# Attention with a top-32 mask: y from the sign tile, reciprocal behind it, scores four steps ahead, turns behind the product with v

## The chip, the cores and the metric

One core of a Trainium2 chip runs the kernel. The metric is device time in microseconds; before the change the median of 3 runs is 1154.14 us (1153.25 to 1154.17). The profile is of one further execution, with a span of 1156.5 us.

## The reference

Attention over 8 batches and 8 heads, 576 positions, head size 64. For each query only the scores not below the 32nd largest count. The result, as 4608 tokens of 512 features, goes into a mixture of 8 experts with a capacity of 80 tokens each.

```
scores = scale * q @ k.T
kth    = 32nd largest of each row of scores
attn   = softmax(where(scores >= kth, scores, -1e9))
x      = (attn @ v), heads side by side            # 4608 x 512
expert = argmax(x @ w_gate); of each expert the 80 tokens of largest gate weight are kept
out    = gate_w * (relu(x @ w1[e]) @ w2[e])        # 0 for the others
```

## The kernel before, in words

**Tiling.** Two heads are taken together: 32 head pairs n. A pair has four full row tiles t = 0 to 3 (128 query rows of two heads) and a tail tile t = 4 (64 rows of each head in one tile of 128). A full tile is two *units*, one a head (h = 0 and 1); the tail is one unit (h = 2). So a pair is nine units and there are 288. A unit is a matrix of 128 rows by 576 scores in f32.

**What is done with a unit.**

- `turn` (L169, L170, L180): TensorE turns q and k of a pair (natural layout) and ScalarE copies them out as qT and kT.
- `front` (L192, L197): TensorE forms the scores of a tile (two units) in a PSUM tile of four banks, of which there is one (`ps_s`, by `four()`); ScalarE copies them, scaled by 2^-48, into an SBUF tile `s`. The turns and the gate logits use the same PSUM tile.
- `parts` (L204): VectorE takes the top 8 of each of six chunks of 96, which makes 48 candidates, in six instructions (the letters G of the step).
- `search` (L215, L223): three rounds of max and match_replace on the candidates give the 24th value w9[7]. Behind the last round ScalarE forms `sign` = Sign(w9[7] - s) with its sum `cnt` (L220), which tells how many scores lie below. VectorE then forms y (L226), s where s < w9[7] and 0 elsewhere; takes y's top 8 (L228); and picks by `cnt` which of the nine values is the 32nd (`pick`, L231). That goes into `thr_all`.
- `below` (L239): GpSimd (POOL) compares s with the threshold: `mask`.
- `turn_w` (L271, L276, L278, L280): TensorE transposes s into PSUM (`ab`, one buffer, and `cc`, two), subtracts the mask by a product with `minus`, and ScalarE takes exp of it: wT.
- `back` (L294): the product of wT with v and a column of ones, into `cc`; the last column holds the sums of the softmax.
- `over` (L306): VectorE takes the reciprocals of the sums, z. `divide` (L315): ScalarE scales the product by them, xn.
- `norm` (L321 to L341): xn is stored, turned, and multiplied by the gate's weights (logits, L332), in pieces spread over steps.

**The order.** It is written out by hand (`tc.manual_schedule`): each engine executes its instructions in the order in which the program issues them. `run` goes through steps i; each brings one unit into the search and carries earlier units onward. The string of letters in `step` is the order on VectorE: G is one of the six chunk maxima of unit i; a to e are the rounds of the search; y, g and h are y, its max and the pick; m is the mask on POOL, and z the reciprocals. `back` tells for each letter how many units behind i its unit is. After the letters come TensorE's and ScalarE's parts of the step. Before the change: turn_w (unit i-3), divide, then, in steps without scores, the turn of the next pair or a piece of norm, then front (unit i+3) and back (unit i-4).

With nine units in a pair and these distances, some steps hold a turn and the product together, and there the turn stands ahead of the product in TensorE's queue.

**Stages.** Attention runs to about 986 us. The routing follows (selection of 80 tokens an expert, to about 1050 us), then the experts. At the end a branch on `bad` would run a slower version (`lean`), which is not executed with these data.

Of the kernel before, what the change touches and what calls it, by code (L numbers as in the profile page):

```python
# [9 lines left out]
F32 = mybir.dt.float32  # L10
BF16 = mybir.dt.bfloat16
# [3 lines left out]
Alu = mybir.AluOpType  # L15
# [10 lines left out]
def kernel(  # L26
# [11 lines left out]
    nc = tc.nc  # L38
    B, H, S, D = q.shape
# [8 lines left out]
    P = 128  # L48
    HP = H // 2
    NP = B * HP  # L50
    NF = S // P
# [8 lines left out]
    NU = NP * UPP  # L60
# [58 lines left out]
    class Attention:  # L119
# [62 lines left out]
        def front(self, n, t):  # L182

            qT, kT = self.turned[n]
            m = P if t < NF else TL
            i = n * UPP + 2 * t
            ps = self.four()
            for j in range(2):
                for h in range(2):
                    d = slice(D * h, D * h + D)  # L190
                    o = ps[:, 2 * h + j, :HS] if t < NF else ps[TL * h : TL * h + TL, j, :HS]
                    nc.tensor.matmul(o, lhsT=qT[d, t * P : t * P + m], rhs=kT[d, j * HS : (j + 1) * HS], start=True, stop=True)  # L192
            g = 2 if t < NF else 1
            s = self.rows.tile([P, 2 * S], F32, name="s", tag="s", bufs=2 if self.lean else 4)
            for h in range(g):
                self.s[i + h] = s[:, h * S : (h + 1) * S]
            nc.scalar.activation(s[:, : g * S].rearrange("p (j c) -> p j c", c=HS), ps[:, : 2 * g, :HS], Act.Copy, scale=TINY)  # L197
# [10 lines left out]
        def search(self, i):  # L208

            s, cand = self.s[i], self.top[i]  # L210
            top = self.top[i] = self.small.tile([P, G0 // 8 - 1, 8], F32, name="top", tag="top")
            w9 = self.small.tile([P, 16], F32, name="w9", tag="w9")
            for r in range(G0 // 8):
                dst = top[:, r, :] if r < G0 // 8 - 1 else w9[:, :8]
                nc.vector.max(out=dst, in_=cand)  # L215
                if r == G0 // 8 - 1:

                    sign = self.rows.tile([P, S], BF16, name="sign", tag="sign", bufs=1)
                    cnt = self.small.tile([P, 1], F32, name="cnt", tag="cnt")
                    nc.scalar.activation(sign, s, Act.Sign, bias=w9[:, 7:8], scale=-1.0, accum_out=cnt)  # L220
                yield
                if r < G0 // 8 - 1:
                    nc.vector.match_replace(out=cand, in_to_replace=dst, in_values=cand, imm_value=LOW)  # L223
                    yield
            y = self.rows.tile([P, S], F32, name="y", tag="y")
            nc.vector.scalar_tensor_tensor(out=y, in0=s, scalar=w9[:, 7:8], in1=s, op0=Alu.is_lt, op1=Alu.mult)  # L226
            yield
            nc.vector.max(out=w9[:, 8:], in_=y)  # L228
            yield
            pick = self.small.tile([P, TOP_K - G0 + 1], F32, name="pick", tag="pick")  # L230
            nc.vector.scalar_tensor_tensor(out=pick, in0=past, scalar=cnt, in1=w9[:, 7:], accum_out=self.thr[:, i : i + 1],  # L231
                                           op0=Alu.is_equal, op1=Alu.mult)
            yield
# [7 lines left out]
        def search_all(self, i):  # L241

            s = self.s[i]
            top = self.top[i] = self.small.tile([P, TOP_K // 8, 8], F32, name="top", tag="top")
            scr = self.rows.tile([P, S], F32, name="y", tag="y")
            nc.vector.max(out=top[:, 0, :], in_=s)
            for r in range(1, TOP_K // 8):
                nc.vector.match_replace(out=scr, in_to_replace=top[:, r - 1, :], in_values=s if r == 1 else scr,
                                        imm_value=LOW)
                nc.vector.max(out=top[:, r, :], in_=scr)  # L250
            nc.vector.tensor_copy(self.thr[:, i : i + 1], top[:, TOP_K // 8 - 1, 7:8])
# [126 lines left out]
        def run(self, slow):  # L378

            units = []  # L380
            for n in range(NP):
                for t in range(NF):
                    units += [(n, t, 0), (n, t, 1)]
                units.append((n, NF, 2))
            first, second = {}, {}
            later = []
            due = []
            drawn = []
            ready = {}

            def whole(i):

                return 0 <= i < NU and units[i][2] > 0

            def step(i, last):
                if 0 <= i < NU:
                    n, t, h = units[i]
                    if t == 0 and h == 1 and 0 < n and n + 1 < NP:
                        self.load(n + 1, *divmod(n + 1, HP))
                    if t in (1, 3) and h == 0 and slow and n:  # L400
                        slow.pop(0)()
                    if t == 1 and h == 0 and n + 1 < NP:
                        due.append(n + 1)
                    first[i] = self.parts(i)

                back = dict(a=0, b=1, c=1, d=1, e=1, y=1, g=2, h=3, m=3)
                for c in "GhmbGcGdGeGGgazy":
                    if c == "G":
                        if 0 <= i < NU:
                            next(first[i])  # L410
                    elif c == "a":
                        if 0 <= i < NU:
                            next(first[i], None)
                            second[i] = self.search(i)
                            next(second[i])
                    elif c == "z":
                        for u in drawn:
                            self.over(*u)
                    elif c == "m":
                        if 0 <= i - back[c] < NU:  # L420
                            self.below(i - back[c])
                    elif i - back[c] in second:
                        next(second[i - back[c]])
                busy = False
                if whole(i - 3):
                    self.turn_w(*units[i - 3][:2])
                ends = []
                for u in drawn:
                    self.divide(*u)
                    if u[1] == NF:  # L430
                        ends.append(u[0])
                drawn.clear()
                fronts = 0 <= i + 3 < NU and units[i + 3][2] != 1
                if not fronts:
                    if due:
                        self.turn(due.pop())
                        busy = True
                for g in list(later):
                    if ready[g] and (fronts or busy) and not last:
                        continue  # L440
                    busy = busy or ready[g] == 1
                    ready[g] = next(g, None)
                    if ready[g] is None:
                        later.remove(g)
                for n in ends:
                    b, hp = divmod(n, HP)
                    later.append(self.norm(n, b, hp, b % 2, 2))
                    ready[later[-1]] = 0
                if fronts:
                    self.front(*units[i + 3][:2])  # L450
                if whole(i - 4):
                    self.back(*units[i - 4][:2])
                    drawn.append(units[i - 4][:2])

            with tc.manual_schedule():
                self.load(0, 0, 0)
                self.load(1, *divmod(1, HP))
                nc.sync.dma_start(wg, moe_w_gate.rearrange("(c p) e -> p c e", p=P))
                self.turn(0)
                i = -3  # L460
                while i < NU + 5 or later:
                    step(i, i > NU + 5)
                    i += 1
            assert not slow and not due

# [277 lines left out]
```

## Time and profile before

| engine | busy us | share of the span | instructions |
|---|---|---|---|
| PE (TensorE) | 921.9 | 80% | 13262 |
| DVE (VectorE) | 999.5 | 86% | 5218 |
| ACT (ScalarE) | 714.0 | 62% | 1534 |
| POOL (GpSimd) | 520.7 | 45% | 344 |

The shares are means over stages of different kinds, so that the stretches by time matter more than this table. Median distance from one y to the next in attention is 3.25 us, the length of a step. The costliest groups on VectorE are these; a line has engine, operation, output and inputs with their shapes and the count, then busy us and mean ns of one, then the idle time just ahead of the group and what ended it.

```profile
L204 DVE MAX8 cand<-s 128x8 f32<-128x96 f32 x1728 | 395.2, 242 | 8.8 <-ACT s L197 8.8
L215 DVE MAX8 top<-cand 128x8 f32<-128x48 f32 x576 | 108.0, 187 | 0.1
L223 DVE MATCH_REPLACE8 cand<-top,cand 128x48 f32<-128x48 f32 x576 | 107.8, 187 | 0.0
L306 DVE RECIPROCAL z_all<-cc 128x2 f32<-128x2 f32 x128 | 19.8, 155 | 32.8 <-PE cc L294 32.6
```

The last figure of L306 is time in which VectorE stood idle in front of the reciprocals, nearly all of it until the product L294 had ended. (The same instruction on the 64-row tails is a form of its own.)

### The profile page before, as it was taken

Reading aid. Unit: us, or ns where it says so; the run is one execution under the profiler, and the core shown is the slowest. Engines: PE = TensorE matmul, PEld = TensorE weight load, DVE = VectorE, ACT = ScalarE, POOL = GpSimd, SP = SyncE. Lnnn points to the kernel's source line nnn. Section 1 sums busy time; section 2 is a strip of 40 time slices with the busy share of each in tenths; the row PEclk is TensorE's granted clock in tenths of the full one; section 3 lists DMA queues with packets and bytes.
Section 4 is the critical chain, followed back from the end, with each engine's and each line's share of the span. In section 5 each row is a group of like instructions: output and inputs, shape, how many; then the busy total and the mean of one; then the engine's idle time right before and its main releaser. Section 6 shows DMA issues by size and latency. Waiting matters only on the chain.

```text
span 1156.5 us, 35811 instructions
## 1 busy us (share of the span) xinstructions
PE 921.9 (80%) x13262; PEld 753.3 (65%) x13262; DVE 999.5 (86%) x5218; ACT 714.0 (62%) x1534; POOL 520.7 (45%) x344
## 2 busy tenths in 40 slices
PE   6988888888888888888888888888888887207897
PEld 3766766666666666676667676666666666207886
DVE  6999999999999999999899999998999998691011
ACT  4777776777677777767677777776777766100110
POOL 2555554555555545555455545545555455001101
PEclk9999998999999899988999989998999988656999
DMA  4144442323232332332132211111111100402830
GB/s 107 34 115 116 115 116 70 79 79 79 79 79 79 79 79 79 79 79 79 48 81 71 62 33 43 39 42 34 42 43 43 43 12 12 156 0 71 312 128 27
DMA packets 167895, 85.77 MB, mean 74 GB/s; under 512 B 117792, under 2 KB 154656, under 8 KB 167712
## 3 DMA queue, kind: packets, MB, share of 16 engines
q1 hardware_dynamic: 166688, 80.78, 25.4%
q0 software_dynamic: 1024, 2.62, 0.7%
q8 instruction: 106, 1.74, 0.6%
q14 instruction: 77, 0.63, 0.2%
HBM read 63.19 MB, written 20.19 MB: 72 GB/s over the span
## 4 chain that ended last, share of the span: by engine, by line
DVE 49%; PE 26%; issue 12%; ACT 9%; POOL 3%; DMA 0%; SPq 0%; DVEq 0%; POOLq 0%; ACTq 0%
DVE cand L204 17%; PE cc L294 7%; DVE y L226 7%; DVE w L228 6%; DVE cand L223 6%; ACT s L197 4%; DVE top L215 3%; PE yp L651 3%; PE sp L169 3%; ACT wT L280 3%; PE ab L271 3%; POOL mask L239 2%; DVE pick L231 2%; DVE w L215 2%; DVE top L526 1%
## 5 line engine op out<-in xcount | busy, mean ns | idle before, releaser
L239 POOL TENSOR_SCALAR mask<-s,thr_all 128x576 bf16<-128x576 f32 x288 | 496.3, 1723 | 477.7 <-DVE cand L223 453.7
L204 DVE MAX8 cand<-s 128x8 f32<-128x96 f32 x1728 | 395.2, 242 | 8.8 <-ACT s L197 8.8
L220 ACT ACTIVATE sign<-s,w 128x576 bf16<-128x576 f32 x288 | 226.2, 786 | 118.1 <-DVE w L215 114.1
L294 PEld LDWEIGHTS cc<-vb,wT 128*64 128x64 f32 x5760 | 217.5, 149 | 36.9 <-ACT wT L280 20.1
L294 PE MATMUL cc<-vb,wT 128*64 128x65 f32 x5760 | 239.4, 236 | 2.6 <-ACT wT L280 1.1
L226 DVE SCALAR_TENSOR_TENSOR y<-s,w 128x576 f32<-128x576 f32 x288 | 228.8, 794 | 0.2 <-issue 0.2
L228 DVE MAX8 w<-y 128x8 f32<-128x576 f32 x288 | 212.3, 737 | 0.0
L192 PE MATMUL sp<-kT,qT 64*128 64x288 f32 (+1 forms) x1280 | 203.6, 438 | 5.0 <-ACT kT L180 2.5
L271 PE MATMUL ab<-ident,s 128*128 128x128 f32 x1152 | 187.6, 294 | 1.2 <-ACT wT L280 1.2
L197 ACT ACTIVATE s<-sp 128x1152 f32<-128x1152 f32 (+1 forms) x160 | 166.8, 1042 | 16.4 <-PE sp L192 16.2
L271 PEld LDWEIGHTS ab<-ident,s 128*128 128x128 f32 x1152 | 136.5, 149 | 25.8 <-ACT wT L280 14.8
L280 ACT ACTIVATE wT<-ab 128x1024 f32<-128x1024 f32 (+1 forms) x160 | 150.6, 941 | 0.0
L276 PEld LDWEIGHTS <-mask 128*128 128x128 bf16 x1440 | 94.9, 99 | 70.4 <-POOL mask L239 68.1
L192 PEld LDWEIGHTS sp<-kT,qT 64*128 64x128 f32 (+1 forms) x1280 | 106.3, 180 | 43.2 <-ACT s L197 4.1
L278 ACT ACTIVATE wT<-cc 128x256 f32<-128x256 f32 (+1 forms) x160 | 58.8, 368 | 108.8 <-PE cc L276 108.8
L276 PE MATMUL cc<-minus,mask 128*128 128x128 bf16 x288 | 64.4, 223 | 59.2 <-POOL mask L239 59.1
L215 DVE MAX8 top<-cand 128x8 f32<-128x48 f32 x576 | 108.0, 187 | 0.1
L223 DVE MATCH_REPLACE8 cand<-top,cand 128x48 f32<-128x48 f32 x576 | 107.8, 187 | 0.0
L276 PE MATMUL ab<-minus,mask 128*128 128x128 bf16 x1152 | 103.2, 221 | 0.0
L315 ACT ACTIVATE xn<-cc,z_all 128x64 f32<-128x64 f32 (+1 forms) x320 | 82.9, 317 | 1.9 <-DVE z_all L306 1.8
L271 PE MATMUL cc<-ident,s 128*128 128x128 f32 x288 | 81.8, 284 | 0.0
L169 PE MATMUL sp<-ident,xn 128*128 128x128 f32 x128 | 26.4, 341 | 42.5 <-ACT s L197 42.5
(164 smaller groups left out, 861.4 us busy)
## 6 DMA issues: line engine op xcount, KB each, us to landing
w<-in_moe_w_dram SPq DMA_DIRECT2D x32, 512.0 KB, 4.0
w<-in_moe_w_dram SPq DMA_DIRECT2D x8, 2048.0 KB, 13.0
out_dram<-zero SPq DMA_DIRECT2D x9, 1024.0 KB, 5.8
qn<-in_q_dram SPq DMA_DIRECT2D x64, 128.0 KB, 3.8
kn<-in_k_dram SPq DMA_DIRECT2D x64, 128.0 KB, 2.9
vb<-in_v_dram SPq DMA_DIRECT2D x64, 128.0 KB, 2.6
xd<-xn SPq DMA_DIRECT2D x32, 256.0 KB, 2.3
qn<-in_q_dram SPq DMA_DIRECT2D x32, 32.0 KB, 3.4
```

Of the source, the lines that this page charges most:

```text
L192: nc.tensor.matmul(o, lhsT=qT[d, t * P : t * P + m], rhs=kT[d, j * HS : (j + 1) * HS], start=True, stop=True)
L197: nc.scalar.activation(s[:, : g * S].rearrange("p (j c) -> p j c", c=HS), ps[:, : 2 * g, :HS], Act.Copy, scale=TINY)
L204: nc.vector.max(out=cand[:, j, :], in_=s[:, j * S // NG : (j + 1) * S // NG])
L220: nc.scalar.activation(sign, s, Act.Sign, bias=w9[:, 7:8], scale=-1.0, accum_out=cnt)
L223: nc.vector.match_replace(out=cand, in_to_replace=dst, in_values=cand, imm_value=LOW)
L226: nc.vector.scalar_tensor_tensor(out=y, in0=s, scalar=w9[:, 7:8], in1=s, op0=Alu.is_lt, op1=Alu.mult)
L228: nc.vector.max(out=w9[:, 8:], in_=y)
L239: nc.gpsimd.tensor_scalar(self.mask[i], self.s[i], self.thr[:, i : i + 1], None, op0=Alu.is_lt)
L271: nc.tensor.matmul(dst[h][c], lhsT=sc[:, keys[c]], rhs=ident, start=c == 0 or (c == NF and h == 0), stop=False, is_transpose=True, skip_gr ...
L276: nc.tensor.matmul(dst[h][c], lhsT=mk[:, keys[c]], rhs=minus, start=False, stop=True, skip_group_check=True)
L280: nc.scalar.activation(wT[:, : g * NF, :], ab.rearrange("p h c r -> p (h c) r")[:, : g * NF, :], Act.Exp, scale=scale / TINY)
L294: nc.tensor.matmul(cc[r : r + TL, o], lhsT=wT[:, j * NF + c if c < NF else 2 * NF + j, r0 : r0 + TL], rhs=vb[:, c, h, :], start=(c == 0), ...
```

## The change

- y becomes s times sign, a plain product of two tensors: s where it is below the 24th value, 0 at it, -s above, so that the maximum over y is the same as long as the values in question are positive. It no longer needs w9 as a scalar, but needs ScalarE's sign tile. `sign` gets two buffers, y one.
- y, its max, the pick and the mask go one step later (`back` 1, 2, 3, 3 becomes 2, 3, 4, 4), so that a step lies between the issue of the sign and its use. What follows (turn_w, back) goes one step later too.
- The reciprocals (z) stand behind y instead of in front of it.
- The scores are formed four steps ahead instead of three, with five `s` tiles instead of four.
- In a step TensorE's order is turn_w, scores, product, and only then a turn or a piece of norm.
- The loads of q, k and v are issued for pair n+2 in the middle of pair n, where they were issued for n+1 near its start; the turn of the next pair is due two steps earlier.

```diff
-            s = self.rows.tile([P, 2 * S], F32, name="s", tag="s", bufs=2 if self.lean else 4)
+            s = self.rows.tile([P, 2 * S], F32, name="s", tag="s", bufs=2 if self.lean else 5)
...
-                    sign = self.rows.tile([P, S], BF16, name="sign", tag="sign", bufs=1)
+                    sign = self.rows.tile([P, S], BF16, name="sign", tag="sign")
...
-            y = self.rows.tile([P, S], F32, name="y", tag="y")
-            nc.vector.scalar_tensor_tensor(out=y, in0=s, scalar=w9[:, 7:8], in1=s, op0=Alu.is_lt, op1=Alu.mult)
+            y = self.rows.tile([P, S], F32, name="y", tag="y", bufs=1)
+            nc.vector.tensor_tensor(out=y, in0=s, in1=sign, op=Alu.mult)
...
-                    if t == 0 and h == 1 and 0 < n and n + 1 < NP:
-                        self.load(n + 1, *divmod(n + 1, HP))
+                    if t == 2 and h == 1 and n + 2 < NP:
+                        self.load(n + 2, *divmod(n + 2, HP))
...
-                    if t == 1 and h == 0 and n + 1 < NP:
+                    if t == 0 and h == 0 and n + 1 < NP:
                         due.append(n + 1)
...
-                back = dict(a=0, b=1, c=1, d=1, e=1, y=1, g=2, h=3, m=3)
-                for c in "GhmbGcGdGeGGgazy":
+                back = dict(a=0, b=1, c=1, d=1, e=1, y=2, g=3, h=4, m=4)
+                for c in "GhmbGcGdGeGGgayz":
...
-                busy = False
-                if whole(i - 3):
-                    self.turn_w(*units[i - 3][:2])
+                if whole(i - 4):
+                    self.turn_w(*units[i - 4][:2])
...
-                fronts = 0 <= i + 3 < NU and units[i + 3][2] != 1
-                if not fronts:
-                    if due:
-                        self.turn(due.pop())
-                        busy = True
+                busy = 0 <= i + 4 < NU and units[i + 4][2] != 1
+                if busy:
+                    self.front(*units[i + 4][:2])
+                if whole(i - 5):
+                    self.back(*units[i - 5][:2])
+                    drawn.append(units[i - 5][:2])
+                if due and not busy:
+                    self.turn(due.pop())
+                    busy = True
...
-                if fronts:
-                    self.front(*units[i + 3][:2])
-                if whole(i - 4):
-                    self.back(*units[i - 4][:2])
-                    drawn.append(units[i - 4][:2])
```

More of the change, by code (lines that the diff above doesn't have):

```diff
@@ L244, in search_all @@
             top = self.top[i] = self.small.tile([P, TOP_K // 8, 8], F32, name="top", tag="top")
-            scr = self.rows.tile([P, S], F32, name="y", tag="y")
+            scr = self.rows.tile([P, S], F32, name="y", tag="y", bufs=1)
             nc.vector.max(out=top[:, 0, :], in_=s)
@@ L423, in step @@
                         next(second[i - back[c]])
-                busy = False
-                if whole(i - 3):
-                    self.turn_w(*units[i - 3][:2])
-                ends = []
+                if whole(i - 4):
+                    self.turn_w(*units[i - 4][:2])
                 for u in drawn:
                     self.divide(*u)
-                    if u[1] == NF:
-                        ends.append(u[0])
+                ends = [n for n, t in drawn if t == NF]
                 drawn.clear()
-                fronts = 0 <= i + 3 < NU and units[i + 3][2] != 1
-                if not fronts:
-                    if due:
-                        self.turn(due.pop())
-                        busy = True
+                busy = 0 <= i + 4 < NU and units[i + 4][2] != 1
[7 more added lines that the diff above has]
+                    busy = True
                 for g in list(later):
-                    if ready[g] and (fronts or busy) and not last:
+                    if ready[g] and busy and not last:
                         continue
@@ L459, in run @@
                 self.turn(0)
-                i = -3
-                while i < NU + 5 or later:
-                    step(i, i > NU + 5)
+                i = -4
+                while i < NU + 6 or later:
+                    step(i, i >= NU + 6)
                     i += 1
```

## The prediction

> **What bounds the kernel now.** I read the 40 slices and the table of stretches first, then who waited for whom, then the groups of VectorE (DVE), then the timeline around one wait.
>
> ```profile
> PE   6988888888888888888888888888888887207897
> DVE  6999999999999999999899999998999998691011
> 300.00:600.00 300.00, 250.93 (x3393) 202.06 (x3395) 290.05 (x1579) 216.69 (x466) 154.82 (x94) 0.94 0.28 75
> ```
>
> Slices are 28.9 us each. Up to about 986 us (slice 34) attention runs with DVE at nine tenths; behind it come routing and the experts, which the change does not touch. In 300 us of attention (PE, weight loads, DVE, ACT, POOL in that order) DVE is busy 290 us, PE 251, ACT 217. So DVE sets the pace, and what shortens it or its pauses shortens the run one for one, 168 us of later stages apart. Who waits, from 12 to 980 us:
>
> ```profile
> ACT wT L278 <- PE cc L276: 106.3, 125, 3.8
> PE sp L169 <- ACT s L197: 50.3, 48, 1.4
> PE sp L332 <- ACT s L197: 42.7, 30, 1.4
> DVE z_all L306 <- PE cc L294: 28.1, 37, 1.4
> ```
>
> Columns: total us, times, longest. DVE has one wait of weight: 37 times the reciprocal L306 stands until the product with v (L294) is done. PE loses more, but at the turns (L169) and gate logits (L332), waiting for ACT to empty the score bank. The timeline joins the two:
>
> ```profile
> 316.29 1.24 PE L192 MATMUL sp<-kT,qT 64*128 64x288 f32 x8
> 316.45 1.02 ACT L280 ACTIVATE wT<-ab 128x1024 f32<-128x1024 f32 x1
> 317.75 1.15 ACT L197 ACTIVATE s<-sp 128x1152 f32<-128x1152 f32 x1
> ...
> 318.96 0.66 PE L169 MATMUL sp<-ident,qn 128*128 128x128 f32 x4 [0.39 <-ACT s L197]
> ...
> 320.54 1.39 PE L294 MATMUL cc<-vb,wT 128*64 128x65 f32 x40
> ...
> 322.04 0.17 DVE L306 RECIPROCAL z_all<-cc 128x2 f32<-128x2 f32 x1 [0.78 <-PE cc L294]
> 322.12 0.80 DVE L226 SCALAR_TENSOR_TENSOR y<-s,w 128x576 f32<-128x576 f32 x1
> ```
>
> The weights wT were ready at 317.47. The product started at 320.54, since the turns of q and k stand ahead of it in PE's queue, and these waited for the score copy until 318.96. Then DVE stood 0.78 us with y queued behind the reciprocal.
>
> **What the Trainium skill says.** (1) "VectorE: DVE Perf Modes", § The TRN2 errata: an fp32 tensor_tensor takes (N+151)/0.96 ns. The trace agrees: 800 elements give 990.6, and L588 below shows 990. (2) The same page, § The perf-mode tier table: tensor_tensor with fp32 has only the 1x rate, so that one bf16 input (sign) brings nothing. L579, whose second input is bf16, takes 488 ns for 320 elements, against 482 for L577. (3) "SBUF — State Buffer", § Who interferes with whom: a DVE instruction with two SBUF inputs shuts out a GpSimd instruction that reads SBUF, and the reverse. Both the old and the new y have two, and POOL's mask (1723 ns) reads s. In the timeline at 505 us pick starts at 505.21, mask runs 505.61 to 507.33, y starts at 507.50: they miss each other by 0.17 us. No run here shows them colliding.
>
> **The change part by part.**
>
> *y by the sign tile.* The rows:
>
> ```profile
> L226 DVE SCALAR_TENSOR_TENSOR y<-s,w 128x576 f32<-128x576 f32 x288 | 228.8, 794 | 0.2 <-issue 0.2
> L228 DVE MAX8 w<-y 128x8 f32<-128x576 f32 x288 | 212.3, 737 | 0.0
> L588 DVE TENSOR_TENSOR hot<-slot,iot 128x800 f32<-128x800 f32 x4 | 3.9, 990 | 3.8 <-PE acc L591 3.7
> ```
>
> A tensor_tensor of 576 is, by (1), 757 ns: 37 ns less than 794. Start to start, which is what the pace feels, the old y takes 0.71 us (507.50 to 508.22, 510.75 to 511.46). Two L588 in a row cover 1.89 us with 0.99 each, so 0.90 apart, 0.067 over their 800/960 us; for 576 that makes 0.667, 0.045 less than 0.71. I take 0.040 x 288 = **11.5 us saved**; ends 0 (the extra time of the old y belongs to something else than its pointer scalar) and 13.
>
> *Its new waits.* y now waits for ACT (the sign) and for DVE (one y buffer: the max L228 of the unit before must have read it). Behind a late y would stand the next unit's searches, then mask, PE's masks and wT. Sign first: it is queued on ACT as soon as L215 has the 24th value. Over the whole attention stage two thirds of the signs started within 0.65 us of that; the late ones in the steady part started up to 3.1 us after it, behind a wT that PE held up (519.77 to 522.60 us is one). 1.0 us covers the sign and its accumulator. But y is moved a whole step later (back of y from 1 to 2), and a step is 3.18 to 3.25 us. Against the y of the following step the tightest sign of the steady part would still have been 1.4 us early, the median 3.2 us. Cost 0; the first steps and the drain apart. The DVE wait: L228 ends at 507.46, y starts at 507.50; instructions that do need the one ahead start 0.04 us after its end (L472 behind L471: 986.64 to 986.68). So it is just met: 0, at most 0.03 x 288 = 9 us. The pick L231 loses two waits of its own in exchange. A second sign buffer keeps ACT from waiting for y.
>
> *Reciprocal behind y.* It moves 0.68 us later at no cost. The 37 waits of at most 1.38 us add to 28.1; each cut by 0.71 leaves 6.5. So this part alone is worth 21.6. ACT's divisions L315 come 0.7 us later, and the sums' bank is held as much longer; the next turn_w into that bank comes two steps after, so it is free.
>
> *Turns behind the product, four steps ahead.* In nine steps (one head pair), the product now stands behind scores or half a turn_w alone, never behind turns or logits. In the case above it would start at 317.5 with wT, 3 us sooner; at the logits (front ends 401.8, logits 403.23, product 403.84) 2 us sooner. Both exceed what is left of any wait. With both parts I take 26 of 28.1 as gone, **26 us saved**, 2 left to irregular steps. The turns then run on while ACT copies scores, so PE's 50.3 + 42.7 us at L169 and L332 shrink too. That is off the path and only gives PE room: 251 us of work in 300 becomes 87% at the faster pace.
>
> *Five s tiles.* Nine units are five tiles, so the scores of a unit reuse the tile of the same place one pair earlier, in the step of that tile's turn_w; ACT's wT of the same step already waits for mask and turn_w ahead of the copy. No new wait. Fronts four ahead are 12.7 us early instead of 9.5; DVE did not wait for scores after the first.
>
> *Loads.* They go out at step 5 of pair n for n+2, with turns at step 1 of n+1: five steps (16 us) instead of two, for transfers that land in 3 to 4 us each. 0.
>
> *Longer pipe.* At the head, the first scores reach DVE as now. At the drain, y, max and pick of the last units have one more step, without search work: from the last L215 (ends 976.03) to the last pick (979.59) the old drain takes 3.6 us, 1.25 of it a wait. Now two y (1.35), three max (1.98) and three picks (0.6) make 3.9, and the last sign, which started 2.2 us after its L215 behind wT, can hold its y about 1 us: **2 us lost**. The drain's own 4.5 and 0.98 us waits stay.
>
> Sum: 1154.1 - 11.5 - 26 + 2 = **1118.6**.
>
> **Rivals.** *A, as above, 1118.6, chance 0.60* (about 1112 to 1124 with the ends of the y cost at 13 and 6 us, no wait left).
> *B, half of it, 1130 to 1135, chance 0.27.* y is no faster, or the single y buffer takes back what it gains (-0), and only the later reciprocal helps: 1154.1 - 21.6 + 2 = 1134.5; with the waits gone but y unchanged, 1130. For it: the 794 of L226 is one form and its pointer is not isolated by any row. Against it: L588 and L577 agree on the pace of tensor_tensor.
> *C, same, 0.03.* New waits of y equal the gain: 35.5 / 288 = 0.12 us each.
> *D, slower, about 1190, chance 0.08.* y meets the mask or the sign in every other step: ACT is blocked in wT up to 3.8 us at a time (106.3 us in total), and the sign stands behind it. 144 steps at 0.5 us are 72 us: 1118.6 + 72 = 1190. For it: the margin to mask is 0.17 us, and DVE's slack goes with its waits. Against it: pick, mask and y keep their distance in the new order (no reciprocal between them now), and sign has a whole step.
> The last 0.02 lie below 1112.
>
> Range 1112 to 1136: A and nearly all of B. Faster 0.89, same 0.03, slower 0.08.
>
> **What would show it.** L226 as TENSOR_TENSOR at 757 ns (right) or 790 (wrong); L306's wait at 0 to 3 us before the drain; DVE at 99% from 300 to 600 us; y with no wait for ACT's sign; waits of L169 and L332 for the score copy below half; attention ending at about 951 us. The forecast is wrong if y shows idle time ahead of it, for sign or with no releaser (POOL's mask), or if L306 still waits.

## The result, and the profile after

The changed kernel takes 1141.03 us (1140.03 to 1142.08) against 1153.70 beside it: a ratio of 0.9891, 95% interval 0.9874 to 0.9908. It is faster by about 12.7 us, where 35.5 were forecast. The time lies above the forecast range.

Almost all that the forecast wanted to see is there. The two rows of slices, and the stretch from 300 to 600 us (PE, weight loads, DVE, ACT, POOL):

```profile
PE   5888888888888888888888988888888887108897
DVE  4999999999999999999999999999999997791011
...
300.00:600.00 300.00, 257.91 (x3471) 201.82 (x3472) 299.41 (x1621) 220.01 (x478) 159.76 (x100) 0.96 0.29 76
```

VectorE is busy 299.4 of 300 us; it was 290. Some of the waits from 12 to 960 us (total us, times, longest):

```profile
DVE y L226 <- ACT sign L220: 4.0, 4, 2.4
PE sp L169 <- ACT s L197: 1.4, 2, 1.2
```

The reciprocals L306 have no wait left before the drain, the last steps of attention (26.8 us before, over the same stretch); the turns L169 wait 1.4 us where they waited 50.3, and the logits L332 are gone from the list. The first line is new: y waits for the sign four times, 4.0 us, of which 3.7 us lie in three waits before 30 us. The new y has its length too (output and inputs with their shapes, busy us, mean ns of one, idle time ahead):

```profile
L226 DVE TENSOR_TENSOR y<-s,sign 128x576 f32<-128x576 f32 x288 | 218.9, 760 | 4.6 <-ACT sign L220 4.0
```

So VectorE hardly pauses and its y is shorter, and yet a step without a reciprocal takes 3.22 us where it took 3.18. Attention ends at about 969 us (the last reciprocal starts at 968.61, before the change at 985.97) and not at 951. A busy share of 99.8% doesn't tell that no time is lost, since records of neighbouring instructions overlap. The starts tell it. First the kernel before, then the changed one, VectorE's timeline (start us, duration us):

```profile
506.73 0.73 DVE L228 MAX8 w<-y 128x8 f32<-128x576 f32 x1
507.39 0.18 DVE L215 MAX8 top<-cand 128x8 f32<-128x48 f32 x1
507.50 0.79 DVE L226 SCALAR_TENSOR_TENSOR y<-s,w 128x576 f32<-128x576 f32 x1
```

```profile
504.45 0.73 DVE L228 MAX8 w<-y 128x8 f32<-128x576 f32 x1
505.11 0.18 DVE L215 MAX8 top<-cand 128x8 f32<-128x48 f32 x1
505.29 0.76 DVE L226 TENSOR_TENSOR y<-s,sign 128x576 f32<-128x576 f32 x1
505.97 0.25 DVE L204 MAX8 cand<-s 128x8 f32<-128x96 f32 x1
```

L228 to L215 is 0.66 us in both. From L215 to y it was 0.11 us and is 0.18; over all units the medians are 0.109 and 0.187, with hardly any spread (0.182 to 0.191 from the 10th to the 90th percentile). The 0.18 us record of L215 just fills the gap, so that no idle time shows. From y to the next instruction it is 0.68 us instead of 0.72. A step gains 0.04 and loses 0.078; 288 times 0.078 are 22.5 us, nearly what is missing. (The expectations below have 0.075 and 21.6, from figures rounded to 0.01 us.)

What stands between L215 and y shows in the list of line 226 (count, then shortest, median and longest ns, then first and last start; DVEq marks an instruction of VectorE's sequencer, which is not counted as busy time of the engine):

```profile
L226 DVE TENSOR_TENSOR y<-s,sign x288: 757/759/899, 19.7 to 960.4; 128x576 f32<-128x576 f32 x144
L226 DVEq EVENT_SEMAPHORE  x287: 21/21/21, 22.7 to 960.3; - x144
```

y has two waits: for ScalarE's sign, and for its own engine, whose L228 must have read the single y buffer. One of them is carried by y itself; for the other there is a semaphore instruction of its own, 287 times. (The Trainium skill says in "Perfetto Trace Analysis", § Identifying Dependency Chains, that an instruction that waits on several engines may have such instructions put ahead of it; it gives no cost.) It is the own-engine wait that stands there: in every one of the 287 cases the trace has the semaphore instruction start 0.04 us after the end of L228 (505.23 after 505.19 in the lines above), and y follows 0.07 us later, except where it waits for the sign. The theories to be told apart: **1**, this pair is the cost: the sequencer stands at the semaphore until L228 has ended and only then issues y; **2**, a wait for the own engine two instructions back costs as much in any form; **3**, the wait for ScalarE, or the sign tile, costs it.

### The profile page after: what moved, and what is told of

The parts are those of the page before. It is cut to its first block, busy times and chain, and to the rows that moved or that the text cites. A ratio compares the mean times of both kernels' runs of the same rounds, so it can differ in the third digit from the quotient of the medians.

```text
span 1139.4 us, 35818 instructions
## 1 busy us (share of the span) xinstructions
PE 925.6 (81%) x13262; PEld 736.9 (65%) x13262; DVE 1005.9 (88%) x5218; ACT 709.8 (62%) x1534; POOL 519.8 (46%) x344
## 4 chain that ended last, share of the span: by engine, by line
DVE 83%; PE 12%; ACT 2%; issue 1%; POOL 1%; DMA 0%; SPq 0%; POOLq 0%; DVEq 0%; ACTq 0%
DVE cand L204 23%; DVE y L226 18%; DVE w L228 16%; DVE cand L223 9%; DVE top L215 6%; PE yp L647 3%; DVE pick L231 3%; DVE w L215 3%; DVE top L522 1%; DVE z_all L306 1%; PE sp L192 1%; PE acc L587 1%; PE cc L294 1%; DVE mg L524 1%; POOL mask L239 1%
## 5 line engine op out<-in xcount | busy, mean ns | idle before, releaser
L204 DVE MAX8 cand<-s 128x8 f32<-128x96 f32 x1728 | 400.2, 246 | 8.9 <-ACT s L197 8.9
L294 PEld LDWEIGHTS cc<-vb,wT 128*64 128x64 f32 x5760 | 213.5, 146 | 65.1 <-ACT wT L280 42.9
L294 PE MATMUL cc<-vb,wT 128*64 128x65 f32 x5760 | 236.2, 233 | 2.7 <-ACT wT L280 2.7
L226 DVE TENSOR_TENSOR y<-s,sign 128x576 f32<-128x576 f32 x288 | 218.9, 760 | 4.6 <-ACT sign L220 4.0
L192 PE MATMUL sp<-kT,qT 64*128 64x288 f32 (+1 forms) x1280 | 210.0, 449 | 14.7 <-ACT part L338 6.1
L228 DVE MAX8 w<-y 128x8 f32<-128x576 f32 x288 | 213.8, 743 | 0.0
L271 PE MATMUL ab<-ident,s 128*128 128x128 f32 x1152 | 175.9, 281 | 1.5 <-ACT wT L280 1.5
L271 PEld LDWEIGHTS ab<-ident,s 128*128 128x128 f32 x1152 | 127.8, 142 | 25.0 <-ACT wT L280 15.6
L215 DVE MAX8 top<-cand 128x8 f32<-128x48 f32 x576 | 110.8, 192 | 0.1
L223 DVE MATCH_REPLACE8 cand<-top,cand 128x48 f32<-128x48 f32 x576 | 110.7, 192 | 0.0
L276 PE MATMUL ab<-minus,mask 128*128 128x128 bf16 x1152 | 110.0, 220 | 0.0
L231 DVE SCALAR_TENSOR_TENSOR pick<-past,cnt,w 128x9 f32<-128x9 f32 x288 | 61.0, 212 | 0.0
## 6 DMA issues: line engine op xcount, KB each, us to landing
w<-in_moe_w_dram SPq DMA_DIRECT2D x8, 2048.0 KB, 11.5
```

The costliest lines, as they stand in the source:

```text
L204: nc.vector.max(out=cand[:, j, :], in_=s[:, j * S // NG : (j + 1) * S // NG])
L226: nc.vector.tensor_tensor(out=y, in0=s, in1=sign, op=Alu.mult)
L271: nc.tensor.matmul(dst[h][c], lhsT=sc[:, keys[c]], rhs=ident, start=c == 0 or (c == NF and h == 0), stop=False, is_transpose=True, skip_gr ...
L276: nc.tensor.matmul(dst[h][c], lhsT=mk[:, keys[c]], rhs=minus, start=False, stop=True, skip_group_check=True)
L294: nc.tensor.matmul(cc[r : r + TL, o], lhsT=wT[:, j * NF + c if c < NF else 2 * NF + j, r0 : r0 + TL], rhs=vb[:, c, h, :], start=(c == 0), ...
```

## Experiments

### One wait, for the own engine: the old y with one buffer

```diff
-            nc.vector.tensor_tensor(out=y, in0=s, in1=sign, op=Alu.mult)
+            nc.vector.scalar_tensor_tensor(out=y, in0=s, scalar=w9[:, 7:8], in1=s, op0=Alu.is_lt, op1=Alu.mult)
```

> The changed kernel with y formed as before, by scalar_tensor_tensor from s and the 24th value, and still one y buffer: y waits for its own engine (the max L228 ahead must have read the one buffer) but no longer for ScalarE, so that it has one wait, carried by the instruction itself. In the changed kernel y starts 0.19 us after the max L215 ahead of it, where 0.11 was expected; 0.075 us x 288 units are 21.6 us. Theory 1, two waits: the second wait makes a semaphore instruction of its own ahead of y, which stands until L228 has ended, and y is issued only then; with one wait the gap is 0.11 us, and the time is 1141.0 - 21.6 + 11.5 for the dearer y = 1131 us. Theory 2, the wait for the own engine costs this much in any form: gap 0.19, time 1141.0 + 11.5 = 1152.5 us. Theory 3, the wait for ScalarE or the sign tile costs it: gap 0.11, 1131 us.

Measured: 1134.33 us, ratio 0.9835 (0.9818 to 0.9851). The median gap is 0.12 us: theory 2 is out, and the own-engine wait alone costs about 0.01 us here. The dearer operation with one wait is faster than the cheaper one with two. The time stays 3 us above the 1131 of theory 1; y itself became longer, which more than covers that:

```profile
L226 DVE SCALAR_TENSOR_TENSOR y<-s,w 128x576 f32<-128x576 f32 x288 | 236.3, 820 | 0.1
```

The mean of 820 ns is some 25 ns more than the 794 of the same instruction in the kernel before, where it had two buffers; from start to start it is 0.02 us more, 5 us in all.

### One wait, for ScalarE: y in place over an f32 sign tile

The plainest control, the changed kernel with a second y buffer, was not run. Instead the y buffer was taken away, and y is written over the sign tile, of which there are two:

```diff
-                    sign = self.rows.tile([P, S], BF16, name="sign", tag="sign")
+                    sign = self.rows.tile([P, S], F32, name="sign", tag="sign")
...
-            y = self.rows.tile([P, S], F32, name="y", tag="y", bufs=1)
+            y = sign
             nc.vector.tensor_tensor(out=y, in0=s, in1=sign, op=Alu.mult)
```

> The changed kernel with the sign tile in f32 and y written over it in place, so that there is no y buffer to wait for: y waits for ScalarE alone. (ScalarE's sign in turn waits for the max over the tile of two units before, up to 1 us later in the step than now.) Theories 1 and 2 (two waits; own-engine wait): gap from L215 to y 0.11 us, 1141.0 - 21.6 = 1119.5 us, the time that was forecast for the change. Theory 3 (the wait for ScalarE or the read of its tile costs it): gap 0.19, 1141 us. Should the later sign hold up wT and the product, the reciprocals L306 wait again and the time lies between the two.

Measured: 1112.82 us (1112.21 to 1114.56), ratio 0.9647 (0.9629 to 0.9664). The gap is 0.11 us in nearly all units, so the wait for ScalarE alone costs nothing: theory 3 is out as far as the wait goes. (The sign tile is f32 here; the bf16 tile is dealt with in the next run.) It is the fastest kernel of the study, 28 us below the changed one and 41 below the one before. It is also 6.7 us below what was expected from the gap alone, and the row says where from:

```profile
L226 DVE TENSOR_TENSOR sign<-s,sign 128x576 f32<-128x576 f32 x288 | 212.2, 737 | 3.6 <-ACT sign L220 3.6
```

y takes 737 ns instead of 760, and 0.657 us from start to start instead of 0.676, which is 5.5 us over 288 units. ScalarE's sign does start later: it waits 174 us in total for L228, and TensorE's product 59.7 us for wT. None of it reaches VectorE before the drain.

### Two waits with something in between: reciprocals in front of y

```diff
-                for c in "GhmbGcGdGeGGgayz":
+                for c in "GhmbGcGdGeGGgazy":
```

> The changed kernel with the reciprocals in front of y again (turns behind the product are kept). Theories 1 and 2: in the 160 steps with a reciprocal the max L228 has ended by the time that y's turn comes, so that the gap of 0.075 us goes there: 1141.0 - 12 = 1129 us. Theory 3: the extra gap stands ahead of y in all steps, 1141 us. Rival on the other side: the reciprocal reads the product 0.68 us earlier in the step and waits again as before the change (28.1 us over 37 times there): 1150 us or more. By the order on TensorE the product should end 3 us ahead of it, so no such wait is expected.

Measured: 1130.61 us, ratio 0.9800 (0.9782 to 0.9817), 10.4 us below the changed kernel. Both kinds of step stand next to each other in VectorE's timeline:

```profile
503.24 0.19 DVE L215 MAX8 top<-cand 128x8 f32<-128x48 f32 x1
503.35 0.15 DVE L306 RECIPROCAL z_all<-cc 128x2 f32<-128x2 f32 x1
503.43 0.76 DVE L226 TENSOR_TENSOR y<-s,sign 128x576 f32<-128x576 f32 x1
...
506.45 0.19 DVE L215 MAX8 top<-cand 128x8 f32<-128x48 f32 x1
506.64 0.76 DVE L226 TENSOR_TENSOR y<-s,sign 128x576 f32<-128x576 f32 x1
```

L215 to y takes 0.19 us with the reciprocal in it and 0.19 without: the reciprocal costs nothing. In the changed kernel it lengthens its step by 0.066 us; 157 steps make 10.4 us, the measured difference. The number is as expected, the way is not. That L228 would have ended by y's turn is not what the trace shows: in the steps with a reciprocal too the semaphore instruction starts 0.04 us after the end of L228, and y 0.10 us after it, as in the others. The reciprocal fills the pause and does not end it. These steps also show that the bf16 sign tile costs y no time at its start: y starts 0.08 us behind the reciprocal, against 0.07 in the kernel before, where y did not read the sign.

A semaphore instruction that is met early is another matter. The kernel before has one for most of its picks:

```profile
L231 DVEq EVENT_SEMAPHORE  x256: 21/21/21, 18.3 to 979.5; - x128
```

In the step of that kernel shown above, the semaphore instruction for the pick runs at 507.50, and the pick starts at 508.39. The pick starts 0.17 us behind the instruction ahead of it, and so it does in the changed kernel, where it has no semaphore instruction. So it is not the semaphore instruction that costs, but standing at it.

L306 has no wait before the drain either, but for 0.1 us: with the other edits in place, the reciprocals need not be behind y.

### The new operation with the own-engine wait alone

```diff
-            nc.vector.tensor_tensor(out=y, in0=s, in1=sign, op=Alu.mult)
+            nc.vector.tensor_tensor(out=y, in0=s, in1=s, op=Alu.mult)
```

> The changed kernel with y = s times s instead of s times sign (the sign tile is still formed for its count; the values picked are then others, and so the masks): the same tensor_tensor and the one y buffer, but y waits only for its own engine, as one wait carried by the instruction. It parts the two waits from the operation. Theory 1 (two waits, of which one becomes a semaphore instruction that holds the sequencer until L228 has ended): gap from L215 to y 0.11 to 0.12 us instead of 0.19, 1141.0 - 0.07 x 288 = 1121 us. Theory 2' (a tensor_tensor behind an own-engine wait has it, whatever the other wait): 0.19 us, 1141 us. Beside it: y takes 737 ns in place and 759 with its own single buffer; if the bf16 sign is the reason it takes 737 here (start to start 0.66), if the single buffer is, 759 (0.68).

The sign no longer enters y, so that thresholds and masks have other values; the instructions and their shapes are the same.

Measured: 1118.29 us (1117.86 to 1119.08), ratio 0.9679 (0.9662 to 0.9695). The gap is 0.12 us:

```profile
504.42 0.19 DVE L215 MAX8 top<-cand 128x8 f32<-128x48 f32 x1
504.54 0.76 DVE L226 TENSOR_TENSOR y<-s 128x576 f32<-128x576 f32 x1
```

The same tensor_tensor and the same single buffer, with one wait in place of two, save 22.7 us: 0.071 x 288 = 20.4 us from the gap and 4.0 us from the waits for the sign, which are gone here too, less 2.4 us that L306 waits more, which makes 22.0. (By the ratios to the kernel before, run beside each, it is 24 us.) Here y starts 0.03 us after the end of L228, where with two waits it was 0.10. Each of the two waits alone costs 0 to 0.01 us, both together 0.08, and in the trace the semaphore instruction starts only when L228 has ended: that leaves theory 1. y takes 758 ns with two f32 inputs, so that the bf16 sign is not why it took 759.

### The two edits of order, alone and together, in the kernel before

Reciprocals behind y:

```diff
-                for c in "GhmbGcGdGeGGgazy":
+                for c in "GhmbGcGdGeGGgayz":
```

> The kernel before with one edit, the reciprocals behind y; turns still ahead of the product, y from the 24th value, two y buffers, three steps ahead. The forecast gave this part 21.6 us: of the 37 waits (28.1 us) what exceeds 0.71 us is left, 6.5 us, so 1153.7 - 21.6 = 1132 us. Rival: the pauses are not lost but come back at other steps, because a DVE that doesn't pause gets further ahead of a PE whose order has not changed: 1140 to 1150 us.

Measured: 1142.01 us, ratio 0.9899 (0.9882 to 0.9915): 11.7 us, about half of the 21.6 forecast for this part. Before 960 us L306 still waits 14.4 us, against 6.5 forecast:

```profile
DVE z_all L306 <- PE cc L294: 14.4, 20, 1.2
```

So the waits did not just shrink by 0.71 us each; some came back, as the rival had it.

Turns behind the product:

```diff
+                if fronts:
+                    self.front(*units[i + 3][:2])
+                if whole(i - 4):
+                    self.back(*units[i - 4][:2])
+                    drawn.append(units[i - 4][:2])
                 if not fronts:
                     if due:
                         self.turn(due.pop())
                         busy = True
...
-                if fronts:
-                    self.front(*units[i + 3][:2])
-                if whole(i - 4):
-                    self.back(*units[i - 4][:2])
-                    drawn.append(units[i - 4][:2])
```

> The kernel before with one edit: in each step scores and product come first on TensorE, turns and pieces of norm behind them; reciprocals in front of y as before, three steps ahead, y from the 24th value. By the forecast the product is then 2 to 3 us earlier in every step with a turn, more than any of the 37 waits: 28 us in the profile, about 1153.7 - 26 = 1128 us. Rival, from the run with the reciprocals alone (1142.0, where 14 us of waits were left): the pauses come from TensorE being late on the whole, and come back at other steps: 1140 us or more.

Measured: 1156.84 us (12 runs) against 1155.29 beside it, ratio 1.0015 (1.0005 to 1.0025). Nothing is gained; it is rather 1.6 us slower. L306 from 12 to 960 us:

```profile
DVE z_all L306 <- PE cc L294: 26.8, 28, 2.3
DVE z_all L306 <- ACT sign L220: 4.5, 2, 2.3
```

These 30 waits are 31.3 us, more than the 27 before, and every one stands at the tail tile of a pair. Some of what happens around one of them:

```profile
323.97 0.64 ACT L180 COPY kT<-sp 128x576 f32<-128x576 f32 x1
...
324.67 1.24 PE L192 MATMUL sp<-kT,qT 64*128 64x288 f32 x8 [1.27 <-ACT kT L180]
...
325.84 1.38 PE L294 MATMUL cc<-vb,wT 128*64 128x65 f32 x20
...
327.32 0.16 DVE L306 RECIPROCAL z_all<-cc 64x2 f32<-64x2 f32 x1 [0.66 <-PE cc L294]
```

The turn of q and k no longer holds up its own step's product. It holds up the scores of the next step, which need the one score bank that ScalarE is still emptying; and in that step the tail's product stands behind the scores. The wait has moved from three places in the pair (the products of t = 1, 2 and 3) to one. In the changed kernel, with nine steps from scores to product instead of seven, the step behind the turn of q and k holds scores but no product, and the step with both scores and the tail's product comes three steps behind the turn (a turn starts at 312.80 us, the tail's product at 322.60).

Both together:

> The kernel before with both edits of order: turns behind the product, and reciprocals behind y. Three steps ahead, four s tiles, y from the 24th value with two buffers and no wait. No wait of L306 before the drain, 28.1 us less than before at most; if the profiled run of before had some 4 us more of them than its timed runs have, 24: 1126 to 1130 us. If four steps ahead and the later y are needed to keep TensorE in time, part of the wait stays: 1133 us or more.

Measured: 1129.67 us (1128.48 to 1131.79), ratio 0.9772 (0.9755 to 0.9788): 25.6 us. Before 955 us, 5.0 us of waits are left in 4 places. So the two edits of order gain 11.7 us and nothing alone, and 26 together. That is the sum that the forecast gave them, in other shares. For the rest of the change (four steps ahead, y and what follows a step later, the loads) little of VectorE's waits is then left: it clears the last 5 us, or, as above, allows the reciprocals in front of y. Which part of it does so was not tried.

## Why the prediction failed, point by point

- **Bound by VectorE, waits of L306 to go**: right. They went wholly (2 us were still allowed for), and both edits without the rest give 25.6 us where 26 was used. The shares were wrong: 21.6 us for the reciprocals alone is 11.7, and "Both exceed what is left of any wait", of the turns, was read off single steps without asking what the moved turns would hold up next. That the sum came out right all the same is in part luck.
- **The cheaper y**: right. The estimate of 757 ns measured 759 (median), and from start to start it is 0.68 us against 0.72: the 0.04 x 288 = 11.5 us were there. One support was weaker than it read: L579 is a scalar_tensor_tensor and L577 reads a PSUM tile, so that 488 against 482 ns tells nothing of a bf16 input to tensor_tensor. The run with y = s times s does (758 against 759).
- **The DVE wait of y** is the step that failed: "it is just met: 0, at most 0.03 x 288 = 9 us". It cost 0.078 x 288 = 22.5 us. The estimate came from L472 behind L471, 0.04 us from end to start; y has two waits, and started 0.10 us after the end of L228, behind a semaphore instruction that waited for it. With one wait the step's 0 to 0.01 us holds (0.12 us gap in two kernels). "The pick L231 loses two waits of its own in exchange" weighed them as equal. The pick's semaphore was met early (0.9 us ahead in the step shown); it cost nothing, and taking it away gained nothing.
- **The wait for sign**: no wait in the steady part but 0.3 us, where 0 was forecast. "The first steps and the drain apart" left out 4.0 us. The drain cost 0.9 us where 2 were charged (from the last w9 to the last reciprocal 9.9 us before, 10.8 after).
- **The rivals**: B named the single y buffer, as something that takes back what y gains. It took back nearly twice that. D's clash of y and mask did not come.

Sum: 1118.6, with 22.5 for the gap, 4.0 for the sign, 2 less of irregular waits and 1.1 less at the drain, is 1142.0 against 1141.03. It agrees better than it should: the profiled execution of before took 1158.3 us and its timed ones 1154, so that the waits taken from the profile may be up to 4 us too many.

## What to carry to other kernels

Count the waits of an instruction and not only whether each is met. Here the second one became a semaphore instruction, and since what it waited for ended just then, 0.07 us came on top of each y; where it was met early, as at the pick, it cost nothing. The wait for the own engine came from saving a buffer. It went away when y was written in place, and a short independent instruction in the pause cost nothing. And an edit of order is judged with what the moved work will hold up in the following step; two edits that each gain little can gain all together.

## What was unexpected in the hardware

- Two waits, of which the semaphore's is met at the last moment: 0.19 us from L215 to y, against 0.11 to 0.12 with one wait (for either engine). Counted from the end of L228, y starts 0.10 us later with the pair, against 0.03 us where it carries the one wait for L228 itself. No idle time shows, since the record of L215 covers it.
- y takes about 25 ns longer (medians) into its single buffer (759 and 758 as tensor_tensor, 819 as scalar_tensor_tensor) than in place over the two sign tiles (734) or into two alternating buffers (794), and 0.02 us more from start to start. Neither the bf16 input nor the number of waits explains it, since 758 and 819 were measured without that input and with one wait. All four kernels with one y buffer write y into the buffer that L228 has just read; that was not tried alone, and the cause stays open.
